# The second MoE of an attention + MoE + MoE kernel, run over its features in four parts

## The chip, the core and the metric

The kernel runs on one core of a Trainium2 chip. The metric is device time in microseconds (us). The engines are TensorE (PE, matmuls and weight loads), VectorE (DVE), ScalarE (ACT), GpSimd (POOL) and SyncE (SP, which issues most DMAs). SBUF is the on-chip memory, PSUM the accumulators of the matmuls (here 4 banks `mm` and 2 pairs of banks `s`).

## The reference, cut to what matters

Attention over 4 batches of 12 heads, 448 positions and 64 columns, then two MoE layers (1792 tokens, 768 columns, 2048 features) on its output. The weights of both MoEs come as float64, the rest as float32.

```python
q_n, k_n = rmsnorm(q, g_q), rmsnorm(k, g_k)
attn = softmax(q_n @ k_n.T / sqrt(64))         # per batch and head
x  = (attn @ v).transpose(0, 2, 1, 3).reshape(1792, 768)
h  = x @ w_in1;   x2 = (h * sigmoid(1.702 * h)) @ w_out1
h2 = x2 @ w_in2;  out = (h2 * clip(h2 + 3, 0, 6) / 6) @ w_out2
```

## The kernel before, in words

All large products run in float16 with each operand split into a high and a low half (`split`, lines 427 to 441: a high half by `scaled`, line 404, and a subtraction for the low one, line 425). A product then is three matmuls: high by high, low by high, high by low (`PROD`).

**Order.** Every step is an `op` of a planner (`Plan`): a set of engines on which it may run with a cost in ns, the steps that it depends on, and leases of buffers from rings. `order()` simulates the engines, picks by rank, and writes one fixed order for each engine; `off`, `pw` and the other constants in `CFG` shift the ranks. At run time each engine goes through its list in order. The matmuls of the MoEs follow one another in program order by a chain of dependencies (`last[0]`). Where the planner foresees a longer gap on PE it puts matmuls of no use into it (line 1488).

**Stages.** For batch 0 the attention runs first, with the weights of the first MoE loaded and decoded beside it. Then for each batch b: its inward product (`add_in1`, line 1218: 16 feature blocks of 128, 448 columns each, 18 matmuls a block), the attention of batch b+1 beside it (`add_norm`, `add_units`; scores in lines 1011 and 1014, products with V in line 972), and its outward product (`add_out1`, line 1271), whose result x2 goes to DRAM (`x2d`). The norm of batch b+1 uses the same SBUF (`arena`) as the turned exponentials of batch b, so it starts after the products with V of batch b. In the trace the inward products run at full pace from about 161, 355, 529 and 695 us, and the second MoE from 808 us.

**Decoding a float64 weight** (`decoded`, lines 496 to 557): one piece of 768 or 1024 values per partition is loaded raw (`wr`, ring of 2), POOL takes the sign (line 525), DVE puts in the low mantissa bits (532), POOL or ACT rebias the high word (516, 521), DVE puts it in (539), giving float32 in `wc` (ring of 2). ACT squares it for its size, DVE makes a scale of it, and `split` writes the halves.

**The second MoE's weights** (`Parked`, lines 605 to 681) are decoded like that while batches 1 to 3 are worked on, 12 pieces of 1024 for w_in2 and 16 of 768 for w_out2, by rows of 128 inputs (one scale per input row and partition). The halves are stored to DRAM (`park`), and loaded back whole into `wa` and `wb`, the homes of the first MoE's weights, once the last batch's products have read those (`add_back`).

**The second MoE** takes 5 chunks of 384, 384, 384, 384 and 256 tokens. Per chunk: x2 is loaded from DRAM and split (`add_x2`, line 1354), 16 feature blocks go inward (line 1218), ACT computes the gate (1364), DVE multiplies (1367) and splits g into `gt` (high half in 410, low in 425). Then for each 128 tokens all 16 features go outward into a pair of PSUM banks (line 1385: 96 matmuls of 384 columns), and ACT or DVE copy both halves out (1404), which are stored.

Of the kernel before, what the change touches and what calls it, by code (L numbers as in the profile page):

```python
# [34 lines left out]
    pw=[1850, 3255, 5600, 4119],  # L35
    pn=[2931, 3150, 2550, 4100],
    ps=[2514, 2461, 2150, 4173],
# [5 lines left out]
    off=[2000, 6000, 10500, -18500, -50000, 30000, -10000, -3000, -3000, 21500, -4500, -12000, -7500, -10000, -43000, -7500, -2000, -2000, -20000, 0],  # L43
    abias=1400,
    cuts=[],
    bias0=[0, 200, 500, 300, 0],
    bias1=[0, 600, 900, 0, 0],
    dlook=1000,
    warm=9,
    late=800,  # L50
    idle=1000,
)
# [52 lines left out]
class Ring:  # L105


    def __init__(self, n, ordered=True):
        self.held, self.ordered, self.made, self.given = [None] * n, ordered, 0, 0

# [3 lines left out]
    def when(self, lease):  # L114

        if self.ordered and lease.turn != self.given:
            return None
        free = [(0.0 if l is None else l.free, i) for i, l in enumerate(self.held) if l is None or not l.todo]
        return min(free) if free else None


class Lease:
    def __init__(self, ring, readers=1):
        self.ring, self.left, self.turn = ring, readers, ring.made
        ring.made += 1


class Op:
# [3 lines left out]
    def __init__(self, ways, deps, takes, gives, dma):  # L132
        self.ways, self.takes, self.gives, self.dma = ways, takes, gives, dma
        self.deps = [d for d in deps if d is not None]
        self.also, self.soft, self.off, self.slack = [], None, 0.0, 0.0
        self.succ, self.rank = [], 0.0


class Plan:
# [48 lines left out]
    def order(self):  # L188
# [5 lines left out]
        for o in self.ops:  # L194
            o.missing, o.ready = len(o.deps), [0.0] * 5
            for l in o.also + [x for x in (o.takes, o.gives) if x is not None]:
                l.todo, l.free, l.slot = l.left, 0.0, None
                l.ring.reset()
# [3 lines left out]
        for _ in self.ops:  # L202
            best = None
            for e in range(5):
                can = []
                for o in wait[e]:
                    r = o.ready[e]
                    if o.takes is not None:
                        free_at = o.takes.ring.when(o.takes)
                        if free_at is None:  # L210
                            continue
                        if free_at[0] + CFG['late'] * (e == PE) > r:
                            r = free_at[0] + CFG['late'] * (e == PE)
# [19 lines left out]
            if o.takes is not None:  # L233
                ring = o.takes.ring
                o.takes.slot = ring.when(o.takes)[1]
                ring.held[o.takes.slot] = o.takes
                ring.given += 1
# [30 lines left out]
    def keep_busy(self, t0, t1):  # L268
# [4 lines left out]
        held = self.spare.held  # L273
# [15 lines left out]
def attention_moe_moe_kernel(ctx, tc, q, k, v, g_q, g_k, w_in1, w_out1, w_in2, w_out2, out):  # L289
    nc = tc.nc  # L290
    B, NH, S, D = q.shape
    NT, DM = out.shape
    DF = w_in2.shape[1]
# [7 lines left out]
    CHUNKS = (384, 384, 384, 384, 256)  # L301
# [10 lines left out]
    def tiles(name, n, shape, dt):  # L312
        return [sb.tile(shape, dt, name=f"{name}{i}") for i in range(n)], Ring(n)

    wa = sb.tile([128, 2, KD, DF], F16, name="wa")
    wb = sb.tile([128, 2, KF, DM], F16, name="wb")
    gt = sb.tile([128, 2 * KF * S], F16, name="gt")
    xt = sb.tile([128, 2, KD, S], F16, name="xt")
    arena = sb.tile([128, 12 * TB * 128], F16, name="arena")
    pt = arena.rearrange("p (s t c) -> p s t c", s=12, t=TB)  # L320
    wr_t, wr_ring = tiles("wr", 2, [128, 1024], I64)
    wc_t, wc_ring = tiles("wc", 2, [128, 1024], I32)
    wbf = wb.rearrange("p e k c -> p (e k c)")

    w1_t, w1_ring = [wbf[:, 10752 + 1536 * i:12288 + 1536 * i].bitcast(I32) for i in range(8)], Ring(8)
    st_t, st_ring = tiles("st", NST, [128, S], F32)
    st_ring.ordered = False
    vr = sb.tile([128, 2, TB, D], F32, name="vr")
    vr_t, vr_ring, pair_ring = [vr[:, i] for i in range(2)], Ring(2), Ring(1)
    qkt_t, qkt_ring = tiles("qkt", 4, [128, 21, 64], F16)  # L330

    vhl, vhl_ring = sb.tile([128, TB, 4, D], F16, name="vhl"), Ring(1)
    bot_t, bot_ring = tiles("bot", 1, [128, S], F16)
    ident16 = sb.tile([128, 128], BF16, name="ident16")
    p_t, p_ring = tiles("p", 8 - NST, [128, S], F32)
    phl, phl_ring = tiles("phl", 2, [128, 2, TB, 128], F16)
    p_ring.ordered = phl_ring.ordered = False
    mm_t, mm_ring = [ps.tile([128, 512], F32, name=f"mm{i}") for i in range(NMM)], Ring(NMM, False)
    s_t, s_ring = [ps.tile([128, 2, 512], F32, name=f"s{i}") for i in range(4 - NMM // 2)], Ring(4 - NMM // 2)
    xd = [dram.tile([KD, 128, 2 * S], F16, name=f"xd{i}") for i in range(2)]  # L340
# [3 lines left out]
    smalls = sb.tile([128, 716], F32, name="smalls")  # L344
# [99 lines left out]
    three = small()  # L444
# [10 lines left out]
    def gains():  # L455
        nc.sync.dma_start(out=gq_t, in_=g_q.unsqueeze(0).to_broadcast([128, D]))
        nc.sync.dma_start(out=gp, in_=g_k.unsqueeze(0).to_broadcast([128, D]))
        nc.gpsimd.memset(three, 3.0)
# [14 lines left out]
    class Weight:  # L473
# [22 lines left out]
        def decoded(self, src, raw, cl, release):  # L496
# [5 lines left out]
            stage = lambda: wr_t[raw.slot].bitcast(F16)[:, :2 * n].rearrange("p (e n) -> p e n", e=2)  # L502
# [44 lines left out]
            done = dict(gives=raw) if release else {}  # L547
# [9 lines left out]
            return c, stage, o  # L557

        def add(self, i, m, after):
# [3 lines left out]
            for j in range(i, i + m):  # L563
                raw, cl = Lease(wr_ring), Lease(self.c_ring)
                flat, _, o = self.decoded(self.src[j], raw, cl, True)
# [39 lines left out]
    class Parked(Weight):  # L605

        def __init__(self, src, inward):
            self.src, self.inward = src, inward  # L610
            self.wide = src.dtype == I64
            self.rows = KD if inward else KF
            self.parts = 2 if inward else 1
            self.n = src.shape[1] // self.parts
            self.sq, self.s = small(self.rows * self.parts), small(self.rows)
            self.e, self.fac, self.emax, self.big_e = small(self.rows), small(self.rows), small(), small()
            self.park = dram.tile([128, 2, self.rows, src.shape[1]], F16, name="park_in" if inward else "park_out")
            self.loads, self.stores, self.scaled = [], [], []
            self.c_t = wc_t

        def add(self, i):
            n, s, e = self.n, self.s[:, i:i + 1], self.e[:, i:i + 1]
            squares, pieces = [], []
            for j in range(self.parts):
                raw, cl = Lease(wr_ring), Lease(wc_ring)
                c, stage, o = self.decoded(self.src[128 * i:128 * i + 128, j * n:j * n + n], raw, cl, False)
                sq = self.sq[:, i * self.parts + j:i * self.parts + j + 1]

                def square(c=c, stage=stage, sq=sq):
                    nc.scalar.activation(out=stage()[:, 0], in_=c(), func=AF.Square, accum_out=sq)  # L630

                squares.append(op((ACT, t_act(n, 1) + 45, square), [o]))
                pieces.append((c, stage, raw, cl))
            m = self.sq[:, i * self.parts:i * self.parts + 1]

            def scale():
                if self.parts == 2:
                    nc.vector.tensor_tensor(out=m, in0=m, in1=self.sq[:, 2 * i + 1:2 * i + 2], op=ALU.add)
                root_exponent(e, m)
                inverse(s, e, 13)  # L640

            o = op((DVE, 480 if self.parts == 1 else 630, scale), squares)
            self.scaled.append(o)
# [778 lines left out]
    for j, n in enumerate(CHUNKS):  # L1422
        chunks.append(Chunk(j, c0, n))
        c0 += n
# [104 lines left out]
```

## Time and profile before

| | before |
|---|---|
| median of 3 runs | 1239.22 us (1237.36 to 1239.52) |
| span of the profiled execution | 1245.9 us |
| PE busy | 1145.1 us (92%) |
| DVE busy | 757.2 us (61%) |
| ACT busy | 705.1 us (57%) |
| POOL busy | 393.6 us (32%) |
| mean granted TensorE clock | 0.977 |

The profiled execution has no time of its own beside its span; the span is 6.7 us over the median of the timed runs. Busy time of PE contains matmuls that wait inside the pipeline, so it is compared with counts of matmuls below. In the rows "in_moe_w_in_dram" and "in_moe_w_out_dram" stand for the weights of both MoEs; 1024-value pieces of w_in and 768-value pieces of w_out belong to the second.

### The profile page before, as it was taken

Reading aid. Unit: us, or ns where it says so; the run is one execution under the profiler, and the core shown is the slowest. Engines: PE = TensorE matmul, PEld = TensorE weight load, DVE = VectorE, ACT = ScalarE, POOL = GpSimd, SP = SyncE. Lnnn points to the kernel's source line nnn. Section 1 sums busy time; section 2 is a strip of 40 time slices with the busy share of each in tenths; the row PEclk is TensorE's granted clock in tenths of the full one; section 3 lists DMA queues with packets and bytes.
Section 4 is the critical chain, followed back from the end, with each engine's and each line's share of the span. In section 5 each row is a group of like instructions: output and inputs, shape, how many; then the busy total and the mean of one; then the engine's idle time right before and its main releaser. Section 6 shows DMA issues by size and latency. Waiting matters only on the chain.

```text
span 1245.9 us, 19206 instructions
## 1 busy us (share of the span) xinstructions
PE 1145.1 (92%) x7151; PEld 654.0 (52%) x7151; DVE 757.2 (61%) x1326; ACT 705.1 (57%) x1512; POOL 393.6 (32%) x340
## 2 busy tenths in 40 slices
PE   2888898889797999989998899999999999999998
PEld 0555544444353455435454455566666666666684
DVE  7998799989889977699768775451041041041040
ACT  3888767888857787557778665541141141141140
POOL 6656667674747323456311221200000000000000
PEclk9999799999999999989999999999999999999999
DMA  6775567799986799866799876470100100100101
GB/s 177 209 192 175 175 193 205 170 193 221 224 261 185 186 193 229 262 188 191 155 193 247 240 252 225 137 215 14 47 18 13 46 19 14 40 12 13 26 1 26
DMA packets 253182, 180.05 MB, mean 145 GB/s; under 512 B 195488, under 2 KB 240544, under 8 KB 250016
## 3 DMA queue, kind: packets, MB, share of 16 engines
q1 hardware_dynamic: 251904, 177.66, 54.7%
q10 hardware_dynamic: 1184, 1.16, 0.4%
q8 instruction: 56, 0.92, 0.3%
q14 instruction: 38, 0.31, 0.1%
HBM read 96.01 MB, written 37.36 MB: 107 GB/s over the span
## 4 chain that ended last, share of the span: by engine, by line
PE 56%; DVE 8%; DMA 4%; issue 3%; ACT 2%; POOL 2%; SPq 1%; ACTq 0%; DVEq 0%; POOLq 0%
PE mm L1218 23%; PE s L1385 18%; PE mm L1271 10%; DMA arena<-phl 2%; PE mm L972 2%; DVE phl L425 1%; PE s L1011 1%; PE s L1014 1%; DVE smalls L782 1%; DMA arena<-in_q_dram 1%; POOL phl L440 1%; DVE arena L836 1%; DVE gt L425 1%; DVE st L1252 1%; ACT p L1024 1%
## 5 line engine op out<-in xcount | busy, mean ns | idle before, releaser
L1218 PEld LDWEIGHTS <-wa 128*128 128x128 f16 x2592 | 255.4, 99 | 193.4 <-issue 15.7
L1271 PE MATMUL mm<-gt,wb 128*128 128x448 f16 x1152 | 231.8, 356 | 10.1 <-POOL wb L440 4.0
L1218 PE MATMUL mm<-xt,wa 128*128 128x448 f16 x1152 | 231.0, 359 | 8.3 <-DVE st L1252 5.4
L1218 PE MATMUL mm<-arena,wa 128*128 128x384 f16 (+1 forms) x1440 | 219.6, 315 | 0.0
L1385 PE MATMUL s<-wb,gt 128*128 128x384 f16 x1344 | 219.2, 326 | 0.0
L1367 DVE SCALAR_TENSOR_TENSOR st<-st,mm 128x384 f32<-128x384 f32 (+1 forms) x80 | 42.1, 527 | 250.3 <-ACT st L1364 250.3
L1385 PEld LDWEIGHTS <-gt 128*128 128x128 f16 x1344 | 131.5, 98 | 86.8
L1271 PEld LDWEIGHTS <-wb 128*128 128x128 f16 x1152 | 112.6, 99 | 119.2 <-issue 6.1
L425 DVE SCALAR_TENSOR_TENSOR gt<-st,smalls,gt 128x448 f16<-128x448 f32 (+2 forms) x144 | 102.5, 717 | 51.7 <-ACT gt L410 50.5
L1024 ACT ACTIVATE p<-s,smalls 128x448 f32<-128x448 f32 x168 | 120.9, 721 | 17.6 <-DVE phl L425 6.6
L1404 ACT ACTIVATE p<-s,smalls 128x384 f32<-128x384 f32 x28 | 14.7, 577 | 199.6 <-PE s L1385 126.8
L410 ACT ACTIVATE gt<-st,smalls 128x384 f16<-128x384 f32 (+2 forms) x132 | 81.5, 621 | 78.3 <-DVE st L1367 46.0
L1019 DVE TENSOR_REDUCE smalls<-s 128x2 f32<-128x896 f32 (+1 forms) x96 | 92.0, 964 | 20.2 <-PE s L1014 19.7
L416 POOL TENSOR_SCALAR arena<-p,smalls 128x384 f16<-128x384 f32 (+1 forms) x13 | 9.9, 761 | 280.5 <-DMA p<-x2d 192.1
L1011 PE MATMUL s<-qkt 128*128 128x448 f16 (+1 forms) x192 | 62.9, 371 | 34.5 <-ACT p L1024 27.5
L1364 ACT ACTIVATE st<-mm,smalls 128x384 f32<-128x384 f32 (+1 forms) x80 | 51.7, 648 | 65.8 <-PE mm L1218 62.9
L425 DVE SCALAR_TENSOR_TENSOR phl<-p,smalls,phl 128x448 f16<-128x448 f32 x90 | 76.4, 875 | 9.6 <-ACT phl L410 5.7
L525 POOL TENSOR_SCALAR wc<-wr 128x1024 f32<-128x1024 f32 (+1 forms) x40 | 45.1, 1128 | 103.2 <-DMA wr<-in_moe_w_out_dram 75.2
L532 DVE SCALAR_TENSOR_TENSOR wc<-wr,wc 128x1024 uint32<-128x1024 uint32 (+1 forms) x40 | 46.9, 1171 | 31.7 <-POOL wc L525 31.7
L1014 PE MATMUL s<-qkt 128*128 128x448 f16 (+1 forms) x192 | 62.4, 366 | 0.0
L440 POOL TENSOR_TENSOR phl<-p,phl 128x448 f16<-128x448 f32 x31 | 43.4, 1409 | 49.4 <-ACT phl L410 43.4
L1073 PE MATMUL mm<-vhl,p 128*128 128x128 f32 x336 | 48.2, 299 | 9.5 <-ACT arena L1083 4.0
(165 smaller groups left out, 1566.1 us busy)
## 6 DMA issues: line engine op xcount, KB each, us to landing
wr<-in_moe_w_in_dram SPq DMA_DIRECT2D x16, 768.0 KB, 4.9
wr<-in_moe_w_out_dram SPq DMA_DIRECT2D x12, 1024.0 KB, 6.2
wr<-in_moe_w_in_dram SPq DMA_DIRECT2D x12, 1024.0 KB, 6.7
wr<-in_moe_w_out_dram SPq DMA_DIRECT2D x16, 768.0 KB, 4.7
qkd<-arena SPq DMA_DIRECT2D x18, 672.0 KB, 3.9
park_in<-wr SPq DMA_DIRECT2D x12, 512.0 KB, 4.4
park_out<-wr SPq DMA_DIRECT2D x16, 384.0 KB, 3.3
wa<-park_in SPq DMA_DIRECT2D x4, 1536.0 KB, 8.9
```

The costliest lines, as they stand in the source:

```text
L410: nc.scalar.activation(out=dst(), in_=src(), func=AF.Copy, scale=s)
L425: nc.vector.scalar_tensor_tensor(out=dst(), in0=src(), scalar=s, in1=high(), op0=ALU.mult, op1=ALU.subtract)
L440: (POOL, t_pool2(n), lambda: nc.gpsimd.tensor_tensor(out=lo(), in0=src(), in1=hi(), op=ALU.subtract)),
L1011: nc.tensor.matmul(o, lhsT=x[:, 64 * t:64 * t + m], rhs=x[:, 448:896], start=True, stop=False)
L1014: nc.tensor.matmul(o, lhsT=x[:, 64 * t:64 * t + m], rhs=x[:, 896:1344], start=False, stop=True)
L1019: nc.vector.tensor_reduce(out=nb, in_=s_t[sl.slot][:, :m, :S], axis=AX.X, op=ALU.max)
L1024: nc.scalar.activation(out=p(i), in_=s_t[sl.slot][:, i, :S], func=AF.Exp, bias=nb[:, i:i + 1], scale=alpha, accum_out=z[:, i:i + 1],)
L1073: nc.tensor.matmul(mm_t[tl.slot][:, 128 * j:128 * j + 128], lhsT=p(i)[:, c:c + 128], rhs=diag(), start=True, stop=True,)
L1218: nc.tensor.matmul(mm_t[ml.slot][:, :n], lhsT=w.inw(we, kc, f), rhs=x[:, xe, kc, :n], start=(kc == 0 and i == 0), stop=(kc == KD - 1 and i ...
L1271: nc.tensor.matmul(mm_t[ml.slot][:, :S], lhsT=W2.outw(we, fc, d * 128, 128), rhs=gv[:, ge_, fc, :], start=(fc == g.part.start and i == 0), ...
L1364: nc.scalar.activation(out=t, in_=m, func=AF.Relu, scale=ch.c3, bias=three)
L1385: nc.tensor.matmul(s_t[sl.slot][:, h, :half], lhsT=g[:, ge_, fc, tb * 128:tb * 128 + 128], rhs=W4.outw(we, fc, h * half, half), start=(fc ...
```

## The change

The second MoE runs over its 2048 features in four parts of 512 (`PARTS` of `PART` = 4 blocks). For each part all 1792 tokens are visited in chunks of 512, 512, 512 and 256. x2 is split once and stays in SBUF for all parts (`x_all`, in the place of `wa`). The outward product of a part is a partial sum: ACT copies it into `acc` (in the place of `wb`) for part 0, DVE adds to `acc` for parts 1 to 3, and the output is stored in part 3.

The weights are no longer parked in DRAM. `Streamed` decodes one part (4 pieces of 768 of w_in2 and 4 of w_out2) into one of two targets, during the part before; part 0 is decoded before the second MoE starts. Its w_in2 pieces may be loaded and brought to 32 bits (ring `uc` of 4) once w_out1 is decoded; its targets lie where the attention worked and are free after the last batch's products with V (`last_users`). w_in2 now is cut by feature blocks (reordered on the host by a reshape), so a scale belongs to a feature; one matmul per part spreads the joint scales of its 8 pieces (`join_scales`).

On PE the outward product of a visit follows the inward product of the next one. Tiles were laid out anew so that these buffers share places, and the planner's constants differ.

```diff
-    CHUNKS = (384, 384, 384, 384, 256)
+    CHUNKS = (512, 512, 512, 256)
...
-    class Parked(Weight):
...
-            return sp(128 * 4 * self.rows * n, load, self.stores + after)
+    PART, PARTS = 4, KF // 4
+    ur_t, ur_ring = row(wr_m, 0, 2, [128, LINE], I64)
+    uc_t, uc_ring = row(wr_m, 12288, 4, [128, LINE], I32)
+    w3_t = [cut(xt_m, 10752, [128, PART, 2, KD, 128], F16), cut(gt_m, 16384, [128, PART, 2, KD, 128], F16)]
+    w4_t = [cut(p_m, 0, [128, PART, 2, DM], F16), cut(gt_m, 28672, [128, PART, 2, DM], F16)]
+    class Streamed:
+        def add(self, part, after, free):
...
+                o = sp(128 * n * (8 if self.wide else 4), load, after, takes=raw)
+                if self.wide:
+                    x = op((POOL, 1.33 * n, sign), [o], takes=cl)
+                    x = op((DVE, t_dve_bits(n), decode_a), [x])
+                    o = op([(POOL, 1.6 * n, rebias_pool), (ACT, t_act(n), rebias_act)], [x])
+                    o = op((DVE, t_dve_bits(n), decode_b), [o])
+                squares.append(op((ACT, t_act(n, 1) + 45, square), [o], gives=raw))
...
+                _, self.done[i] = split(
+                    lambda e, i=i: self.dst(i, e), lambda c32=c32: c32().bitcast(F32), self.s[:, i:i + 1], n,
+                    [o] + free, gives=cl, pool=spread(i, KF, CFG['rw'][2 if self.left else 3]),
+                )
...
+    x_all = cut(wa_m, 0, [128, 2, KD, NT], F16)
+    acc = cut(wb_m, 0, [128, NT // 128, DM], F32)
...
+        def leave(self, wdone, acc_free):
...
+                    if part == 0:
+                        o = op((ACT, t_act(half, 1), first), [last[0], self.sized] + acc_free, gives=sl)
+                    else:
+                        o = op((DVE, t_dve(half) + 85, add), [last[0], added[at, h]], gives=sl)
...
-        if b == 0:
-            for i in range(W3.rows):
-                W3.add(i)
-            W3.add_scales(1.0)
...
+    W3.add(0, sum([w.done for w in (W2,)], []), last_users)
+    W4.add(0, [], last_users)
+    for part in range(PARTS):
+        for j, ch in enumerate(chunks):
+            here = Visit(ch, part, len(visits), joined)
+            here.enter(visits[-2].left_ if len(visits) > 1 else acc_free)
+            visits.append(here)
+            if len(visits) > 1:
+                u = visits[-2]
+                u.leave(None, acc_free)
...
+            if j == 0 and part + 1 < PARTS:
+                W3.add(part + 1, [], [before.entered] if part else acc_free)
+                W4.add(part + 1, [], [before.left] if part else acc_free)
+                following = join_scales(part + 1)
```

## Rows read from the trace of the kernel before

**Rows 1.** The page: its head.

```profile
span 1245.9 us, 19206 instructions
```

**Rows 2.** Windows by stage: length, busy of each engine (instructions), granted clock, DMA.

```profile
355.00:529.00 174.00, 161.99 (x1032) 83.94 (x1031) 145.02 (x239) 126.78 (x290) 77.90 (x64) 0.97 0.88 221
529.00:695.00 166.00, 150.76 (x975) 78.75 (x974) 134.57 (x245) 119.69 (x273) 59.74 (x55) 0.97 0.84 197
695.00:808.00 113.00, 112.50 (x602) 58.87 (x602) 68.02 (x137) 67.02 (x111) 25.28 (x23) 1.00 0.64 215
808.00:1246.00 438.00, 432.23 (x2753) 269.18 (x2751) 102.13 (x195) 118.32 (x198) 7.07 (x9) 1.00 0.13 36
```

**Rows 3.** Windows, two undisturbed stretches of PE.

```profile
748.00:779.00 31.00, 31.00 (x166) 16.05 (x164) 15.50 (x28) 16.32 (x28) 5.83 (x6) 1.00 0.68 226
841.00:872.00 31.00, 31.00 (x193) 18.66 (x191) 4.69 (x8) 6.19 (x10) 0.00 (x0) 1.00 0.06 14
```

**Rows 4.** Timeline of PE: start, length, line, [idle before].

```profile
524.70 4.69 PE L1488 MATMUL mm<-ident 128*128 128x512 bf16 x21
...
801.21 6.01 PE L1218 MATMUL mm<-arena,wa 128*128 128x384 f16 x36
```

**Rows 5.** Windows of line 972, the products with V, by stage.

```profile
529.00:695.00 166.00, 17.34 (x286) 13.21 (x286) 0.97 0.84 197
```

**Rows 6.** Waits of PE from 355 to 695 us: total, times, longest.

```profile
PE s L1011 <- DMA qkt<-qkd: 5.5, 1, 5.5
PE mm L1218 <- DVE st L1252: 4.4, 1, 4.4
```

**Rows 7.** Windows by stage of tile wr, raw weights: DVE, ACT, POOL.

```profile
355.00:529.00 174.00, 29.28 (x22) 11.03 (x16) 22.07 (x15) 0.97 0.88 221
529.00:695.00 166.00, 22.72 (x20) 18.59 (x26) 12.00 (x9) 0.97 0.84 197
695.00:808.00 113.00, 32.98 (x33) 34.08 (x50) 20.22 (x17) 1.00 0.64 215
```

**Rows 8.** Chain of waits in order of time: start, length, what.

```profile
368.35 1.55 DVE wc L532
489.29 7.69 DMA arena<-phl
693.78 0.96 DVE wc L532
```

**Rows 9.** Groups by form: decoding, 355 to 695, then 748 to 800 us.

```profile
L425 DVE SCALAR_TENSOR_TENSOR wr<-wc,smalls,wr 128x1024 f16<-128x1024 f32 x7 | 10.4, 1493 | 0.5 <-POOL wr L416 0.5
...
L539 DVE SCALAR_TENSOR_TENSOR wc<-wr,wc 128x768 int32<-128x768 int32 x7 | 7.3, 1040 | 1.3 <-ACT wr L521 0.8
L425 DVE SCALAR_TENSOR_TENSOR wr<-wc,smalls,wr 128x768 f16<-128x768 f32 x5 | 5.6, 1127 | 4.7 <-ACT wr L410 4.7
L390 DVE TENSOR_SCALAR smalls<-smalls 128x1 int32<-128x1 int32 x7 | 1.1, 153 | 7.0 <-ACT wr L630 7.0
L410 ACT ACTIVATE wr<-wc,smalls 128x768 f16<-128x768 f32 x5 | 4.7, 935 | 2.7 <-DVE smalls L399 2.6
```

**Rows 10.** Groups by form: 529 to 600 us, 748 to 800 us, the page.

```profile
L425 DVE SCALAR_TENSOR_TENSOR gt<-st,smalls,gt 128x448 f16<-128x448 f32 x16 | 13.1, 828 | 1.1 <-POOL gt L416 1.1
...
L425 DVE SCALAR_TENSOR_TENSOR gt<-st,smalls,gt 128x448 f16<-128x448 f32 x2 | 1.4, 677 | 0.0
L532 DVE SCALAR_TENSOR_TENSOR wc<-wr,wc 128x768 uint32<-128x768 uint32 x7 | 6.7, 956 | 16.8 <-POOL wc L525 16.8
...
L425 DVE SCALAR_TENSOR_TENSOR phl<-p,smalls,phl 128x448 f16<-128x448 f32 x90 | 76.4, 875 | 9.6 <-ACT phl L410 5.7
```

**Rows 11.** Waits of SP's queue from 355 to 695 us.

```profile
SPq L509 <- DMA park_in<-wr: 7.2, 5, 2.5
```

**Rows 12.** Groups by form from 808 to 1246 us.

```profile
L1367 DVE SCALAR_TENSOR_TENSOR st<-st,mm 128x384 f32<-128x384 f32 x64 | 35.3, 554 | 196.2 <-ACT st L1364 196.2
```

**Rows 13.** Waits over the span.

```profile
DVE wc L532 <- POOL wc L525: 31.7, 18, 5.9
```

More of the change, by code (lines that the diff above doesn't have):

```diff
@@ L195, in order @@
             o.missing, o.ready = len(o.deps), [0.0] * 5
-            for l in o.also + [x for x in (o.takes, o.gives) if x is not None]:
+            for l in o.also + o.takes + ([] if o.gives is None else [o.gives]):
                 l.todo, l.free, l.slot = l.left, 0.0, None
@@ L232, in order @@
                 wait[w[0]].remove(o)
[L233 to L237, printed above, removed]
+            for l in o.takes:
+                l.slot = l.ring.when(l)[1]
+                l.ring.held[l.slot] = l
+                l.ring.given += 1
             o.way = way
@@ L309, in attention_moe_moe_kernel @@
     queue = lambda: nc.scalar if plan.queue else nc.sync
[L312 to L319, printed above, removed]
+    wa_m = sb.tile([128, 2 * KD * DF], F16, name="wa")
@@ L603, in outw @@
             return wb[:, e, fc, d0:d0 + n]
-    class Parked(Weight):
[L609 to L643, printed above, removed]
-            for j, (c, stage, raw, cl) in enumerate(pieces):
-                _, l = split(lambda k, stage=stage: stage()[:, k], c, s, n, [o], gives=cl, pool=spread(
-                    i * self.parts + j, self.rows * self.parts, CFG['rw'][self.number]))
-                def store(j=j, stage=stage):
-                    queue().dma_start(out=self.park[:, :, i, j * n:j * n + n], in_=stage())
-                self.stores.append(sp(128 * n * 4, store, [l], gives=raw))
-        def add_scales(self, f):
-            lease = Lease(mm_ring)
-            e16 = self.emax.bitcast(BF16)[:, :1]
-            row = lambda: mm_t[lease.slot][:, :128]
-            def largest():
-                nc.vector.tensor_reduce(out=e16, in_=self.e, axis=AX.X, op=ALU.max)
-            def spread_out():
-                nc.tensor.matmul(row(), lhsT=e16.to_broadcast([128, 128]), rhs=ident16, start=True, stop=True)
-            def scales():
-                nc.vector.tensor_reduce(out=self.big_e, in_=row(), axis=AX.X, op=ALU.max)
-                inverse(self.emax, self.big_e, 0)
-                times(self.fac, self.e, self.emax, f)
-            o = op((DVE, 200, largest), self.scaled)
-            o = op((PE, 300, spread_out), [o], takes=lease)
-            self.big = op((DVE, 700, scales), [o], gives=lease)
-        def add_back(self, j, k, after):
-            n = self.src.shape[1] // k
-            here = (wa if self.inward else wb)[:, :, :, j * n:j * n + n]
-            def load():
-                queue().dma_start(out=here, in_=self.park[:, :, :, j * n:j * n + n])
-            return sp(128 * 4 * self.rows * n, load, self.stores + after)
@@ L1362, in add_in2 @@
[L1362 to L1384 removed]
+            self.bs = [batches[b] for b in range(c0 // S, (c0 + n - 1) // S + 1)]
@@ new lines, in gate, with product @@
+                def gate(t=t, m=m, c=c, k3=k3):
+                    nc.scalar.activation(out=t(), in_=m(), func=AF.Relu, scale=c, bias=k3)
+                def product(t=t, m=m, k6=k6):
+                    nc.vector.scalar_tensor_tensor(out=t(), in0=t(), scalar=k6, in1=m(), op0=ALU.min, op1=ALU.mult)
+                o = op((ACT, t_act(n, 2) - 50, gate), [last[0], self.sized], takes=tl)
+                o = op((DVE, t_dve(n), product), [o], gives=ml)
+                o = op(scaled(hi, t, 1.0, n), [o] + g_after)
```

414 lines of the change are left out of this document (283 added, 131 removed).

## The prediction, made before the change was run

> **What bounds the kernel now.** I read the head of the page first [rows 1]: the profiled span is 1245.9 us, 6.7 us over the median of the timed runs, 1239.2, so sums are made against the span and 6.7 us come off at the end. In the windows by stage [rows 2] PE looks like the bound everywhere, but the ends of its matmuls are modelled, so I compared what a stage takes with what its matmuls need at full rate. Full rate is read where nothing disturbs it [rows 3]: 166 matmuls of 448 columns in 31.0 us are 186.7 ns each, 193 of 384 columns 160.6 ns, both 0.417 to 0.418 ns a column.
>
> The second MoE runs at that rate: 1152 + 1344 + 288 matmuls of 384 and 256 columns are 2 x 516,096 columns, 431.7 us, and PE is busy 432.2 in the last stage of 438. The last batch's first MoE does too: 576 x 186.7 = 107.5 us in a stage of 113 that also holds 36 matmuls of the next one (6.0 us) [rows 4]. The two stages from 355 to 695 us don't. Each holds one batch's first MoE (107.5), the next batch's scores (96 matmuls, 17.9) and its products with V (17.3 in the dearer stage [rows 5]): 142.7 us of PE in 174 and 166. That is 54.6 us too much. PE there waits for q/k transposes and DVE's gate product [rows 6], or runs filler matmuls ahead of an inward block [rows 4].
>
> DVE is the reason that I can show: busy 145.0 of 174 and 134.6 of 166 [rows 2]. 52.0 us of that (29.3 + 22.7) are instructions on the raw tile of the second MoE's weights [rows 7], and the chain of waits goes through them by name: between 355 and 695 it has 21 pieces of that decoding, 25.4 us, of which the first and the last stand in [rows 8]; three small scale instructions on DVE beside them add about 3.
>
> **The change, part by part.** *Decoding leaves the attention stages.* DVE loses there the 52.0 us and the small ones, three of 0.153 us for each of 13 pieces [rows 9], 6.0: 58. What comes back is part 0 of w_in2, which has to wait for its target until the last batch's products with V and can only be decoded to 32 bits: four pieces with two passes of 0.96 [rows 10] and 1.04 us [rows 9] and 0.46 of scales, 8.5 us. So DVE needs 279.6 - 58 + 8.5 = 230 us in two stages where PE needs 285.4. The 60.4 us in which DVE now stands idle there are waits for other engines and DMAs. If all of them stay, the stages take 230 + 60.4 = 290.5. If the chain alone shortens, they take 340 - 25.4 - 3 + 8.5 = 320. If all comes off, PE's 285.4 remain. I take 295, near the DVE sum and above it, since two engines would now be near their limit at once: 45 us won, bounds 20 and 55. ACT (126.8 + 119.7, of which 29.6 go) and POOL (77.9 + 59.7, of which 34 go) lose work too and stay under DVE.
>
> A side of this is weighed with the Trainium skill. The row: the same low-half subtraction of 128x448 takes 828 ns from 529 to 600 us, with POOL busy, and 677 from 748 to 800 us [rows 10]. The Trainium skill, "SBUF — State Buffer", section "Who interferes with whom", says that a DVE instruction with two SBUF inputs and a GpSimd instruction that reads SBUF exclude each other for the whole instruction. By that rule the attention's own subtractions would become shorter when POOL loses a quarter of its work there: 32 gate instructions with 0.15 and two thirds of the 90 split ones with 0.20 us too much are 17 us, a quarter of which is an estimated 4 us, and the sum would be 1189. The rows alone show the difference, not its cause, so my sum goes without it.
>
> *The queue.* SP is in order. From 355 to 695 it stood 7.2 us at weight loads whose buffer a parked store still held, with DMA transposes behind them [rows 11]. 28 stores and 6 loads back go. This runs beside the DVE term and is not added to it.
>
> *The stage from 161 to 355* decodes w_out1, and that stays. Two pieces of w_in2 fall into it, each with three passes on DVE, the longest of them 1.49 us, and 0.46 of scales [rows 9]: at most 10 us. Bounds 0 and 10, and I take 5. The new constants of the planner shift the order of all loads; no row prices that, and I put it at 0 with 10 to either side.
>
> *695 to 808.* Here PE has no gap to win. DVE is busy 68.0 of 113, 33.0 of it on the decoding of w_out2 [rows 2, 7]. Afterwards it has four pieces of w_out2 (4 x 3.5 = 14), four subtractions for w_in2 (4.4) and those for x2 (some 17) instead: no more than now. x2's first chunk needs batches 0 and 1 only, and the third chunk, which needs the last batch, is entered three blocks of 15.4 us later. 0.
>
> *The second MoE.* The columns stay 2 x 516,096, so PE's need stays 430.2 to 431.7. DVE gets 84 additions for parts 1 to 3, beside the 28 evacuations that ACT keeps for part 0. An addition reads PSUM and SBUF as the gate product does, 0.55 us [rows 12]: 47 us. Gate products and subtractions keep their columns and stay inside the 102 of now. 24 pieces with 0.96 + 1.04 + 1.13 + 0.46 [rows 9, 10]: 86. 16 visits with three to four scale instructions, some 1 us: 16. Together 251 of 432 us. ACT goes from 118 to some 190: 24 pieces with three passes of 0.94 [rows 9] are 68. All of this lies beside matmuls. What could let it through is the PSUM ring: a feature block of 512 columns takes PE 3.85 us, and with four banks the next three blocks are 11.5 us, against some 1.5 us for gate and product (0.74 for the product in proportion [rows 12], as much for the gate). 24 loads of 768 KB in 330 us are 57 GB/s on DMA engines that are 13% busy there [rows 2]. The matmuls that spread scales stand in PE's queue and wait for eight pieces; I put one wait of about 1 us at each of four parts, well under the single waits in [rows 6], 4 us. At the end two additions (1.1 us) and a store follow the last matmul, where two copies and stores half as large follow now: at most 1 us, inside the 4.
>
> Sum: 1245.9 - 45 - 5 + 4 = 1199.9 of span; less 6.7 is **1193 us**.
>
> **Rivals.** *Only the chain's own pieces go* (17 in 100). The attention stages are a sequence of scores, maximum, exponential, split, transpose, and the last one ends behind DMA transposes of up to 7.7 us [rows 8]; for it speaks that PE's idle and filler time gathers at the ends of batches. Then 20 us are won there and none in the first stage: 1239.2 - 20 + 4 = 1223. Against it: DVE is over 80% busy and runs in order, so every piece taken out moves what is behind it.
>
> *All of it goes, and more* (19). The stages reach PE's need (55 us), and the first stage, 194 us for the same 142.7, gives 20 because w_out1 gets the raw tiles to itself and SP and POOL are freer: 1239.2 - 55 - 20 + 2 = 1166. Against it: w_out1's decoding isn't touched.
>
> *DVE's order lets the streaming through to PE* (10), the case on the other side. DVE executes in order. A first decoding pass that waits for its load and for POOL holds up the gate product behind it, and with it a PSUM bank. Such waits exist: from 748 to 800 us DVE stood 16.8 us before 7 of these passes, 2.4 each [rows 10], and the longest such wait in the run is 5.9 [rows 13]. In a chunk of 256 columns three blocks cover only 5.8 us less some 1 of gate and product. If every one of 24 pieces cost PE its 2.4 us, that is 58: 1193 - 4 + 58 = 1247. It decides from 1.9 us a piece (46 over 24). Against it: the same pieces run today from 695 to 808 beside matmuls, and those lost nothing.
>
> *The decoding still comes early* (2): the planner could load and decode parts 1 to 3 before the attention ends. Four buffers for 32-bit pieces hold part 0 until the last products with V, so it can't go further; no change then, 1239.
>
> My forecast has 52.
>
> **How the numbers follow.** The forecast's own range is 1176 (55 and 10 won, 2 lost) to 1214 (30 won, 5 lost). The range reaches to most of the case of all gains and past that of the chain: 1150 to 1228. Outside are the streaming rival (10), part of the case of all gains (5) and the fourth with some remainder (5). A difference of 0.2%, about 2.5 us, is what runs of this kernel can tell. Slower: 9 of the streaming rival's 10. No change: the early decoding 2, and 2 from the border of the others. Faster: 87.
>
> **What would show it.** Right: stages of about 147 us between inward blocks where 174 and 166 stand; DVE some 25 us less busy in each; no decoding in the chain before the last batch; PE busy in the whole second MoE with waits of at most a few us, DVE at about half. Wrong: PE waits on the gate product or on weights in the second MoE, gaps at the part changes, a lower granted clock there than the 1.00 of now [rows 2], or attention stages as long as before with DVE less busy, which would make them a chain of latencies.

## The result, and the profile after

The changed kernel takes 1193.1 us in the median (1190.0 to 1195.4), the kernel before on the same chip 1239.4 (1237.4 to 1242.9): a ratio of 0.961, 95% interval 0.957 to 0.965. The forecast was 1193 us.

The head of the page, against [rows 1]; the span is 55.2 us shorter:

```profile
span 1190.7 us, 18317 instructions
```

The windows by stage, against [rows 2], with the first stage ahead: length, busy of PE, PEld, DVE, ACT, POOL (instructions), granted clock, share of the DMA engines, GB/s. The edges from 342 us on are the ends of the four batches' outward products.

```profile
161.00:342.00 181.00, 155.87 (x980) 80.35 (x978) 160.69 (x264) 135.94 (x307) 124.67 (x96) 0.93 0.80 199
342.00:491.00 149.00, 144.75 (x965) 76.14 (x964) 109.85 (x196) 114.03 (x269) 45.76 (x49) 0.99 0.82 186
491.00:634.00 143.00, 140.29 (x903) 73.00 (x902) 109.09 (x203) 103.41 (x247) 46.36 (x47) 0.99 0.78 176
634.00:748.00 114.00, 113.76 (x644) 60.13 (x643) 62.87 (x125) 54.15 (x93) 17.89 (x18) 1.00 0.29 97
748.00:1191.00 443.00, 437.22 (x2507) 244.92 (x2505) 222.76 (x395) 145.25 (x237) 56.18 (x44) 1.00 0.16 51
```

These edges are not those of [rows 2], which lie where an inward product came to full pace. By such instants (342.2, 490.6 and 642.4 us) the two attention stages take 148 and 152 us where 174 and 166 stood. Between the ends of outward products, the measure of the table below, they take 148.5 and 143.6 where 151.6 and 163.9 stood, and the last batch 113.9 where 131.9 stood, because the attention of before ran on into the next batch. PE now is busy in nearly all of both stages. The second MoE keeps its length although DVE works 222.8 us in it instead of 102.1.

PE's timeline where batches meet (start, length, line, with [idle before] where there is any) shows it. In both kernels an inward product starts as the outward one ends. In the kernel before it then broke off for filler [rows 4] and for the late products with V of its own batch (line 972), 11 us after it had started in batch 2 and 20 in batch 3:

```profile
505.45 3.00 PE L1218 MATMUL mm<-xt,wa 128*128 128x448 f16 x15
...
516.50 3.12 PE L972 MATMUL mm<-arena,vhl 128*64 128x128 f16 x55
...
689.27 3.19 PE L972 MATMUL mm<-arena,vhl 128*64 128x128 f16 x55 [1.62 <-DMA arena<-phl]
```

In the changed kernel these products (line 1062) end ahead of batch 2's inward product and 6 us behind the start of batch 3's, no filler is left behind 342 us, and the second MoE starts as the last outward product ends:

```profile
486.31 3.21 PE L1062 MATMUL mm<-xt,gt 128*64 128x128 f16 x55 [0.25 <-DMA xt<-p]
489.45 1.31 PE L1361 MATMUL mm<-gt,wb 128*128 128x448 f16 x6
490.60 2.43 PE L1308 MATMUL mm<-xt,wa 128*128 128x448 f16 x12
...
631.73 2.62 PE L1361 MATMUL mm<-gt,wb 128*128 128x448 f16 x13
634.19 3.00 PE L1308 MATMUL mm<-xt,wa 128*128 128x448 f16 x15
637.12 3.12 PE L1062 MATMUL mm<-xt,gt 128*64 128x128 f16 x55
...
642.36 7.92 PE L1308 MATMUL mm<-xt,wa 128*128 128x448 f16 x41 [0.21 <-DVE smalls L423]
...
743.76 4.51 PE L1361 MATMUL mm<-gt,wb 128*128 128x448 f16 x23
748.11 4.26 PE L1479 MATMUL mm<-wa,xt 128*128 128x512 f16 x19
```

PE's waits from 340 to 1190 us (total, times, longest), against [rows 6], are these three; the 5.5 us for the transposes and the 4.4 us for the gate product are gone, and none lies in the second MoE. Over batches 1 to 3 PE's waits were 27.2 us in the profile shown (24.8 in the second profile of the kernel before) and are 7.1; filler matmuls took 17.4 us there (17.3) and now take none.

```profile
PE s L1101 <- ACT p L1114: 6.7, 2, 4.0
PE mm L1062 <- DMA xt<-p: 0.2, 1, 0.2
PE mm L1308 <- DVE smalls L423: 0.2, 1, 0.2
```

The raw tile's instructions by the same windows (length, DVE, ACT, POOL, clock, DMA), against [rows 7]: 6 us of DVE are left in the two attention stages where 52 were (45 between the ends of outward products), and 67.3 have moved into the second MoE.

```profile
342.00:491.00 149.00, 5.96 (x5) 4.59 (x8) 3.19 (x3) 0.99 0.82 186
491.00:634.00 143.00, 0.00 (x0) 0.00 (x0) 0.00 (x0) 0.99 0.78 176
634.00:748.00 114.00, 28.10 (x27) 20.48 (x31) 15.96 (x15) 1.00 0.29 97
748.00:1191.00 443.00, 67.31 (x60) 47.89 (x74) 50.83 (x36) 1.00 0.16 51
```

The page's groups that answer to [rows 12] and [rows 10]: the additions to `acc`, the gate product, and the low-half subtraction of the turned exponentials (mean ns after the busy time).

```profile
L1529 DVE SCALAR_TENSOR_TENSOR wb<-s,smalls,wb 128x384 f32<-128x384 f32 x84 | 48.1, 613 | 88.2 <-PE s L1513 88.1
L1494 DVE SCALAR_TENSOR_TENSOR wa<-wa,smalls,mm 128x512 f32<-128x512 f32 (+1 forms) x64 | 43.4, 678 | 77.6 <-ACT wa L1491 77.3
L458 DVE SCALAR_TENSOR_TENSOR p<-p,smalls 128x448 f16<-128x448 f32 x90 | 71.0, 821 | 17.4 <-ACT p L443 15.6
```

### The profile page after: what moved, and what is told of

It is laid out like the page before. It is cut to its first block, busy times and chain, and to the rows that moved or that the text cites. A ratio compares the mean times of both kernels' runs of the same rounds, so it can differ in the third digit from the quotient of the medians.

```text
span 1190.7 us, 18317 instructions
## 1 busy us (share of the span) xinstructions
PE 1108.2 (93%) x6748; PEld 610.0 (51%) x6748; DVE 804.2 (68%) x1426; ACT 678.6 (57%) x1469; POOL 408.4 (34%) x362
## 4 chain that ended last, share of the span: by engine, by line
PE 67%; DVE 15%; DMA 5%; ACT 5%; POOL 4%; issue 4%; SPq 0%; DVEq 0%; POOLq 0%; ACTq 0%
PE s L1513 18%; PE mm L1479 18%; PE mm L1361 15%; PE mm L1308 7%; PE mm L1062 3%; PE s L1101 2%; PE s L1104 2%; DMA xt<-in_q_dram 2%; DVE gt L458 1%; DVE smalls L1109 1%; DVE smalls L872 1%; DMA xt<-p 1%; ACT p L1114 1%; PE mm L1029 1%; PE mm L1163 1%
## 5 line engine op out<-in xcount | busy, mean ns | idle before, releaser
L1513 PEld LDWEIGHTS <-gt 128*128 128x128 f16 x1344 | 131.6, 98 | 87.3
L1308 PEld LDWEIGHTS <-wa 128*128 128x128 f16 x1152 | 114.0, 99 | 118.3 <-issue 18.1
L1513 PE MATMUL s<-p,gt 128*128 128x384 f16 x672 | 110.8, 326 | 0.0
L1513 PE MATMUL s<-gt 128*128 128x384 f16 x672 | 110.5, 326 | 0.0
L1479 PE MATMUL mm<-wa,gt 128*128 128x512 f16 (+1 forms) x576 | 110.3, 352 | 0.0
L1479 PE MATMUL mm<-wa,xt 128*128 128x512 f16 (+1 forms) x576 | 110.2, 352 | 0.0
L1101 PE MATMUL s<-gt 128*128 128x448 f16 (+1 forms) x192 | 64.4, 382 | 23.5 <-ACT p L1114 20.7
L1479 PEld LDWEIGHTS <-gt 128*128 128x128 f16 x576 | 56.3, 98 | 52.1
L1479 PEld LDWEIGHTS <-xt 128*128 128x128 f16 x576 | 56.2, 98 | 52.1
L458 DVE SCALAR_TENSOR_TENSOR p<-p,smalls 128x448 f16<-128x448 f32 x90 | 71.0, 821 | 17.4 <-ACT p L443 15.6
L443 ACT ACTIVATE p<-p,smalls 128x448 f16<-128x448 f32 (+1 forms) x96 | 60.2, 659 | 9.6 <-DMA xt<-p 6.4
L1104 PE MATMUL s<-gt 128*128 128x448 f16 (+1 forms) x192 | 64.3, 378 | 0.0
L458 DVE SCALAR_TENSOR_TENSOR gt<-wa,gt 128x512 f16<-128x512 f32 (+1 forms) x64 | 42.0, 658 | 25.5 <-ACT gt L443 25.4
```

Of the source, the lines that this page charges most:

```text
L443: nc.scalar.activation(out=dst(), in_=src(), func=AF.Copy, scale=s)
L458: nc.vector.scalar_tensor_tensor(out=dst(), in0=src(), scalar=s, in1=high(), op0=ALU.mult, op1=ALU.subtract)
L1101: nc.tensor.matmul(o, lhsT=x[:, 64 * t:64 * t + m], rhs=x[:, 448:896], start=True, stop=False)
L1104: nc.tensor.matmul(o, lhsT=x[:, 64 * t:64 * t + m], rhs=x[:, 896:1344], start=False, stop=True)
L1308: nc.tensor.matmul(mm_t[ml.slot][:, :n], lhsT=w.inw(we, kc, f), rhs=x[:, xe, kc, :n], start=(kc == 0 and i == 0), stop=(kc == KD - 1 and i ...
L1479: nc.tensor.matmul(mm_t[ml.slot][:, :n], lhsT=W3.inw(we, kc, f), rhs=x_all[:, xe, kc, ch.c0:ch.c0 + n], start=(kc == 0 and j == 0), stop=( ...
```

## The experiments

All runs are compared by the instants at which the outward products of the four batches and the last matmul end. The lengths between them are in us and come from one profiled execution of each kernel; the first column is an instant, and ratios are to the kernel before on the same chip:

| run | batch 0 ends | batch 1 | batch 2 | batch 3 | second MoE | median, ratio (95%) |
|---|---|---|---|---|---|---|
| before, profile shown | 354.0 | 151.6 | 163.9 | 131.9 | 438.8 | 1239.4 |
| before, once more | 345.6 | 152.2 | 162.5 | 129.7 | 438.9 | 1236.4, one run |
| after | 342.3 | 148.5 | 143.6 | 113.9 | 436.9 | 1193.1, 0.961 (0.957 to 0.965) |
| e1 old structure, new constants | 348.5 | 144.6 | 165.0 | 127.0 | 467.2 | 1259.5, 1.014 (1.009 to 1.019) |
| e2 new structure, old constants | 355.8 | 147.2 | 143.2 | 113.6 | 436.9 | 1204.5, 0.970 (0.967 to 0.974) |
| e3 decoding again | 341.7 | 143.0 | 160.1 | 131.6 | 436.9 | 1225.0, 0.986 (0.982 to 0.990) |
| e4 loads again | 342.2 | 143.8 | 164.2 | 113.7 | 436.8 | 1208.2, 0.973 (0.969 to 0.977) |
| e5 DVE passes again | 339.0 | 147.8 | 148.2 | 143.8 | 436.9 | 1223.4, 0.985 (0.981 to 0.988) |
| e6 two banks | 341.3 | 150.6 | 144.5 | 113.9 | 442.5 | 1198.5, 0.963 (0.960 to 0.966) |
| e7 w_out1 without DVE passes | 323.2 | 158.7 | 148.9 | 113.7 | 436.9 | 1190.2, 0.956 (0.953 to 0.959) |
| e9 48 reductions, same order | 342.0 | 159.2 | 148.7 | 113.9 | 436.9 | 1208.8, 0.974 (0.971 to 0.978) |
| e11 24 reductions | 345.1 | 153.6 | 144.5 | 113.9 | 437.0 | 1198.3, 0.966 (0.964 to 0.969) |
| e10 48 in the second MoE | 342.1 | 149.3 | 145.2 | 113.9 | 447.3 | 1204.1, 0.971 (0.969 to 0.973) |
| e12 three engines, same order | 344.9 | 160.3 | 155.0 | 113.9 | 436.9 | 1216.3, 0.980 (0.977 to 0.984) |

**The kernel before, once more.** No edit.

> The kernel before, profiled a second time: its first profile had a span 6.7 us over the median of its runs. If that profile is typical in its stages, batches end again near 354, 506, 670 and 801 us; if the surplus lies in one place, it is gone there and the span is near 1238.

Its profiled span is 1234.6 us, 11.3 less than that of the profile shown, and 8.4 of these lie ahead of the end of batch 0. So these two executions of one kernel differ most in the first stage, and its length alone proves little below some 10 us. Behind it executions agree better: e10 leaves batches 1 to 3 of the changed kernel as they are, and they take 408.4 us where 406.0 stand for the changed kernel. Against the second execution of before the change won 3.3 us in the first stage, 3.7, 18.9 and 15.8 in batches 1 to 3, 2.0 in the second MoE and 0.2 behind it: 43.9. Batches 1 to 3 together went from 444.4 to 406.0, by 38.4 (by 41.4 against the profile shown).

**Structure and constants apart.** e1 is the kernel before with the new planner constants, e2 the changed one with the old:

```diff
-    pw=[1850, 3255, 5600, 4119],
-    pn=[2931, 3150, 2550, 4100],
+    pw=[226, 922, 5600, 4119],
+    pn=[5844, 7048, 2259, 9380],
...
```

> The kernel before with the changed kernel's planner constants (those of the parked weights kept). Theory: the gain of 46 us comes from taking the second MoE's decoding off DVE in the attention stages, so constants alone leave the time near 1239, 1227 to 1250. Rival: the new constants order the attention better and make most of the gain; then it is 1215 or less.

> The changed kernel with the old planner constants for the stages up to the last batch: paces, biases, and the offsets of the values, the norms, the units and the inward products (those of the first batch's norm and units, of the first MoE's weights and of the outward product have to stay new, since no order exists otherwise). Theory: the move itself carries the gain, 1193 to 1212. Rival (constants): 1222 or more.

e2 came as the theory had it: with the old constants batches 1 to 3 take 404.0 us, no more than with the new ones, so what was won there is the structure's. The first stage is 13.5 us longer with them, near to the whole difference of 11. e1 missed both expectations. The new constants shorten batches 1 to 3 of the old structure by 7.8 us and put a hole of 30 us into the start of its second MoE. PE's timeline of e1 there (first two lines) shows it full of filler matmuls, and the chain of waits (last line) goes through them alone:

```profile
784.94 6.01 PE L1218 MATMUL mm<-arena,wa 128*128 128x384 f16 x36
...
790.93 29.51 PE L1488 MATMUL mm<-ident 128*128 128x512 bf16 x136
```

```profile
791.07 29.38 PE mm L1488 x136
```

So the profile shows nothing that PE waited for there; the planner had foreseen a gap and filled it, and the 136 useless matmuls are the loss. Without the 28.3 us by which its second MoE is longer e1 would be at an estimated 1231, inside the theory's range. Constants fitted to one structure are no neutral part of a comparison.

**Decoding, loads and DVE passes put back, with the planner's order made anew.** Each kernel is the changed one with 16 pieces of unused work between w_out1's decoding and part 0: e3 decodes them in full, e4 only loads them, e5 only runs three DVE passes of 768 values and the small scale instructions for each, spread over batches 1 and 2.

```diff
-    W3.add(0, sum([w.done for w in (W2,)], []), last_users)
+    again = [extra(i) for i in range(KF)]
+    W3.add(0, sum([w.done for w in (W2,)], []) + again, last_users)
```

> The changed kernel, with the 16 pieces of w_in2 loaded, decoded and split once more between the end of w_out1's decoding and the last attention, and thrown away: some 56 us of DVE, 25 to 45 of ACT and POOL, 12.6 MB of loads, no parking stores. Theory (DVE's decoding work is what the attention stages lose): most of the 40 us that the two attention stages gained are lost again, 1213 to 1238. Rival (the stages are a chain of latencies, or the gain is that of the parked stores and the loads back): 1203 or less.

> The changed kernel with only the 16 loads of the run before put into the same stages, 12.6 MB into the raw buffers, nothing computed from them. Theory (DVE): nothing to see, 1190 to 1200. Rival (traffic of the DMA queue, whose transposes the attention waits for): 1208 or more.

> The changed kernel with the DVE share of the decoding alone put back into the stages of batches 1 and 2: 16 times three passes over 768 values and the two scale instructions, some 53 us of DVE, on a 32-bit buffer, no loads, nothing on POOL or ACT, each group released by a matmul of the stage (its values are used by nobody). The run with all of the decoding put back lost 30 us, the one with the loads alone 14, of which 13.2 are one wait behind a late store. Theory (DVE): 1210 to 1235, spread over the stages. Rival (the order of SP's queue and the transfers make the loss, DVE's work little): 1203 or less.

e3 gives back 28.7 us of the 38.4 in batches 1 to 3, with the profile of before: batch 1 cheap, 2 and 3 dear. e4 went against the theory by its number, but not by the transposes that the rival had named: 13.2 of its 15.7 us are one wait of PE (first line), and the chain of waits that leads to it (start, length, what) goes through the store of x2. That store stood in SP's queue behind transposes (line 1175) and weight loads (line 664), and ACT needed its buffer `st`.

```profile
PE mm L1112 <- ACT mm L1446: 13.2, 1, 13.2
```

```profile
493.48 0.51 SPq L1175
...
494.79 0.59 SPq L664
...
495.43 5.21 DMA x2d<-st
...
500.66 0.65 ACT st L1427
...
501.81 0.20 ACT mm L1446
...
502.05 4.00 PE mm L1112 x20
```

e5 met its number, but between the ends of outward products batches 1 and 2, where the passes are, lose 3.9 us together and batch 3 loses 29.9. That is an attention that ended late: from the last product with V of batch 1 to that of batch 3 pass 341.8 us in e5, 340.6 in the kernel before, once more, and 307.6 in the changed one. Whether DVE's passes did that isn't isolated: they took turns in the ring of part 0's buffers, so that its real decoding starts at 634.8 us (336.5 in the changed kernel), and the planner made another order. Such runs change order and queues along with the load, so they can't say what DVE's time alone is worth.

**Engine time put back, with no order changed.** In e9, e11, e10 and e12 every engine keeps the changed kernel's order. Only reductions of 128x8x128 values into a private buffer come between DVE's instructions (e12: and small products on POOL and squares on ACT between theirs), from batch 1's first inward block to the last products with V; in e10 from the second visit of the second MoE to its last.

```diff
-        for o in self.done:
...
+        for i, o in enumerate(self.done):
             o.way[2]()
+            if i0 <= i < i1 and o.way[0] == DVE:
+                k += 1
+                if k % 7 == 0 and n < 48:
+                    n += 1
+                    self.more()
```

> The changed kernel with every engine's order as it stands, and 48 reductions of no use on DVE (128x8x128 bf16, an estimated 1.1 us each, some 50 us in all), one after every 7th DVE instruction from batch 1's first inward block to the last batch's products with V. They share no buffer with anything and no other engine gets an instruction. Theory (DVE's time is what the attention stages gained): 24 us more DVE work per stage brings back 15 to 35 us, all of it before the second MoE, so 1208 to 1228 us. Rival (what the runs with added decoding lost came from the planner's other order, from buffers and from SP's queue): at most 1201 us.

> The same with 24 reductions, one after every 14th DVE instruction (some 26 us). Theory: about half of the loss of the run with 48, or somewhat less since PE's and DVE's needs then are closer: 1200 to 1212 us. Rival: at most 1197 us.

> The changed kernel with its order, and on three engines as much time of no use as the change took from them between batch 1's first inward block and the last batch's products with V: the 48 DVE reductions of before (58 us, 1208.8 us by themselves), 88 POOL products of 64 columns (an estimated 50 us) and 114 ACT squares of 64 columns (an estimated 30 us). No transfer, no buffer shared, no other order. If the engines' time is what the stages gained, the kernel comes back to 1220 to 1240 us. Rival (a good part of the gain is in the transfers and in what the decoding's instructions wait for, not in the engines' time): at most 1215 us.

Group of the reductions and windows of batches 1 to 3 in e9; then the same windows in the kernel before, once more:

```profile
L1645 DVE TENSOR_REDUCE smalls<-ident 128x8 f32<-128x1024 bf16 x48 | 58.0, 1208 | 0.0
...
342.00:501.00 159.00, 147.41 (x960) 77.07 (x959) 134.46 (x218) 113.12 (x267) 46.85 (x49) 0.97 0.76 174
501.00:650.00 149.00, 141.51 (x909) 73.53 (x907) 132.23 (x229) 103.85 (x250) 43.10 (x47) 0.98 0.74 169
650.00:764.00 114.00, 113.76 (x644) 60.09 (x643) 62.82 (x125) 54.70 (x93) 18.36 (x18) 1.00 0.30 98
```

```profile
346.00:498.00 152.00, 142.62 (x904) 73.47 (x902) 132.10 (x219) 116.89 (x271) 70.23 (x57) 0.98 0.90 213
498.00:660.00 162.00, 152.45 (x957) 78.79 (x956) 129.75 (x224) 112.93 (x256) 64.73 (x58) 0.97 0.82 203
660.00:790.00 130.00, 123.90 (x714) 65.53 (x713) 83.48 (x167) 79.50 (x141) 28.07 (x27) 0.99 0.72 228
```

e9's DVE is as busy in batches 1 and 2 as that of the kernel before (134.5 and 132.2 against 132.1 and 129.8), but they cost 15.8 us, not 38.4, and batch 3 stays at PE's need. Half of the reductions (e11) cost 6.0 in batches 1 to 3, over twice the 2.4 between two executions; the median of 1198.3 falls between the two ranges. So DVE's time is a cause, at 0.2 to 0.3 us per us, and e9 met the theory's range at its low end. e12 adds 36.2 us on POOL and 28.7 on ACT. In batches 1 and 2 DVE, ACT and POOL then are busy 265, 241 and 123 us where they were 262, 230 and 135 in the kernel before, once more. The cost rises to 23.2 us, and the median, 1216.3, falls between the rival's 1215 and the theory's 1220. Its groups:

```profile
L1654 POOL TENSOR_TENSOR smalls<-gp 128x64 f16<-128x64 f32 x88 | 36.2, 411 | 3.5
L1657 ACT ACTIVATE smalls<-gp 128x64 f16<-128x64 f32 x114 | 28.7, 251 | 2.4
```

So some 60% of what was won in batches 1 to 3 (23.2 of 38.4) comes back with engine time. The other 15.2 us do not, and no run here isolates them. Two things that e12 lacks can be read in the chain of the kernel before, once more, where batches 2 and 3 start:

```profile
503.68 4.43 PE mm L1488 x14
...
676.01 5.38 DMA wr<-in_moe_w_out_dram
681.54 0.90 POOL wc L525
682.46 0.96 DVE wc L532
683.42 0.55 DVE xt L1110
684.00 0.35 PE mm L1218
```

The first is the planner's filler. PE's waits in batches 1 to 3 are 26.0 us in e12 and 24.8 in the kernel before, once more; what e12 lacks are the 69 filler matmuls, 17.3 us. 14 of them stand in the chain themselves: as far as the profile shows nothing else held PE in these 4.4 us. The others fill time in which something else was late.

The second is what a pass waits for. PE waited for `xt`, the attention's result. DVE had that subtraction of 0.55 us in its order behind a decoding pass, and the pass waited for a weight of 5.4 us and for POOL's sign. DVE stood idle for 1.1 us before the pass, which no busy time shows. How much of the 15.2 us each of the two is wasn't isolated, since transfers and the planner's order changed with them.

**The second MoE's cover.** e6 lets its inward product use two of the four `mm` banks; e10 puts e9's 48 reductions there.

```diff
-                ml, tl = Lease(mm_ring), Lease(t_ring)
+                ml, tl = Lease(mm_ring, most=2), Lease(t_ring)
```

> The changed kernel with two PSUM banks in place of four for the inward products of the second MoE, so that one block (3.85 us) covers gate, product and whatever DVE does before them, not three. Theory: the streaming fits between the gate products with much to spare, under 6 us more, 1192 to 1200. Rival (DVE's order lets the decoding through to PE, and four banks just cover it): 1215 or more.

> The same 48 reductions, but put in the second MoE, one after every 5th DVE instruction from its second visit to its last. Theory: DVE is busy half of that stage and four PSUM banks cover a delay of 1.1 us, so at most 4 us are lost: 1192 to 1198 us. Rival (DVE's in-order queue lets delays through to PE there): 1205 us or more.

e6: 5.6 us, inside the theory's range. e10 fell between the two: 10.4 us more in the second MoE, 7.4 of it two waits of PE's outward product for DVE's addition, the longer one in the timeline below. The 48 matmuls behind that wait took 10.51 us, at a granted clock of 0.75 from 905.4 to 915.9 us, where such 48 take 7.96 without a wait ahead of them, so the wait of 6.4 us cost about 9:

```profile
905.38 10.51 PE L1521 MATMUL s<-gt 128*128 128x384 f16 x48 [6.42 <-DVE wb L1537]
```

The windows say why a stage with DVE at half isn't half free. First e10 around that wait, with 6 reductions in it (7.3 us), then the same stretch in the changed kernel, where it lies 2 us earlier, and then a busier one there, 11 us before it:

```profile
875.00:907.00 32.00, 25.58 (x131) 12.74 (x130) 30.92 (x55) 16.79 (x29) 7.37 (x6) 0.95 0.31 107
```

```profile
873.00:905.00 32.00, 32.00 (x175) 16.89 (x174) 25.24 (x45) 14.28 (x24) 8.62 (x6) 1.00 0.39 124
...
862.00:894.00 32.00, 32.00 (x171) 16.50 (x169) 28.72 (x54) 20.14 (x34) 12.87 (x10) 1.00 0.41 138
```

Where a part's pieces are decoded, DVE is 90% busy for 32 us already without the reductions. The addition, last in line, holds one of only two pairs of `s` banks.

**w_out1 without DVE's two passes** (24 passes, 37.0 us of DVE, less in the first stage; neither the low nor the high word is put in, so only the signs of its weights are left).

```diff
-                x = op((DVE, t_dve_bits(n), decode_a), [x])
+                if self.inward:
+                    x = op((DVE, t_dve_bits(n), decode_a), [x])
...
-                o = op((DVE, t_dve_bits(n), decode_b), [o], **done)
...
+                if self.inward:
+                    o = op((DVE, t_dve_bits(n), decode_b), [o], **done)
```

> The changed kernel without the two DVE passes that put the mantissa of the first MoE's outward weights together (12 pieces, 24 passes of 1.2 to 1.4 us; the weights lose their low bits, the rest is unchanged). Theory: the stage before 342 us is bound by DVE as the later ones were, and gives back 15 to 30 us, 1164 to 1180. Rival (a chain of latencies there): under 8 us, 1186 or more.

By its total it fell on the rival's side, by the stage that it is about on the theory's: the first stage is 19.1 us shorter, over twice the 8.4 by which two executions of the kernel before differ there, and batches 1 and 2 are 10.2 and 5.3 longer. The planner made another order for it, so why that was given back isn't shown.

## Why the prediction was right, step by step

- *Attention stages, -45 (bounds 20 and 55), and nothing in the last batch:* -38.4 against the second execution of before, -41.4 against the profile shown. The size held, the reason in part. I took DVE's sum plus its idle time, as if the sum set the stage and the idle stayed. DVE fell from 261.9 us in batches 1 and 2 to 218.9, but e9 gives a us of DVE back at under 0.3 us. The rest is the other engines' share (7.4) and 15.2 us that came back with neither. The case of the chain's pieces, which I had only as a rival, is probably part of them; of its 25.4 us, which I read as DVE's, some 14 are passes on DVE and the others on ACT, POOL and one load. The reading that fits these runs, though none tests it alone, is a race. Where the attention of the next batch ends after the outward product, the time behind goes to waits and filler; where it ends first, PE's need of 142.7 is what is left. The last products with V ended 14 and 23 us behind the outward product in the profile shown, and now end 1 us ahead of it and 6 behind; the stages stand 5.8 and 0.9 above PE's need, the last batch 6.4 above its 107.5.
- *First stage, -5 (0 to 10):* -3.3 against one execution of before, -11.7 against the other. The reason that I gave is not borne out: e2, which moves the same two pieces out of it but has most of the old constants, ends it at 355.8, later than either execution of before.
- *Span against median, -6.7:* right as a correction: 8.4 us of that execution's surplus over the other are in its first stage.
- *Constants at 0, 10 to either side:* e2 puts them at 11 us, just outside, and nearly all in the first stage, in the new structure.
- *Second MoE, +4:* -2.0. The single waits at part changes did not come: the trace has none. DVE is at 222.8 us where I summed 251, half of the stage, as said: the additions took 613 ns, not 550, but four of the 24 pieces were decoded before the stage, and scales, products and subtractions took less. ACT is at 145.3 where I summed some 190.
- *The total.* That it came within 0.2 us is luck. Against the second execution of before 6.6 us less than forecast were won in the attention stages and 1.7 less in the first stage, and 6.0 more in the second MoE, so that the misses nearly cancel.
- *Rivals.* Streaming getting through to PE did not happen, but its place was right: e10 shows the path at `s`, where I had priced `mm` alone. All gains and more (1166) failed in the first stage. The early decoding did not come: the raw tile has no work at all from 491 to 634 us.
- *Signs.* Stage lengths (148 and 152 us between inward products), no waits in the second MoE and DVE at half came as listed. "No decoding in the chain before the last batch" did not quite: four passes of part 0 (4.1 us) stand in it from 343 to 364 us, then none.
- *The side on subtractions.* In batches 1 and 2 the gate's went from 895 ns (32 times, the kernel before, once more) to 813, and the split ones from 864 (71 times) to 724 (78 times): some 13 us, more than the estimated 4. The Trainium skill, "SBUF — State Buffer", "Who interferes with whom", says that a DVE instruction with two SBUF inputs contends with a GpSimd instruction that reads SBUF. By that rule less POOL work would be the cause. e12 doesn't bear that out: with 36.2 us of POOL put back beside e9's load, the gate's mean is 827 against 824, and that of the split ones 692 against 709. Those POOL products are short, and buffers were laid out anew too, so the cause of the shorter time stays open.

The group of the gate's subtractions in batches 1 and 2, in the changed kernel, e9 and e12:

```profile
L458 DVE SCALAR_TENSOR_TENSOR gt<-st,smalls,gt 128x448 f16<-128x448 f32 x32 | 25.5, 813 | 1.7 <-POOL gt L449 1.6
```

```profile
L466 DVE SCALAR_TENSOR_TENSOR gt<-st,smalls,gt 128x448 f16<-128x448 f32 x32 | 26.1, 824 | 1.1 <-POOL gt L457 0.8 <-ACT gt L451 0.2
```

```profile
L467 DVE SCALAR_TENSOR_TENSOR gt<-st,smalls,gt 128x448 f16<-128x448 f32 x32 | 26.1, 827 | 1.9 <-POOL gt L458 1.7 <-ACT gt L452 0.2
```

## What to carry to other kernels

Work that depends on nothing nearby belongs in the stage whose bound it doesn't touch: 67 us of decoding on DVE cost the second MoE nothing that shows, and the stages that had held 52 of them gained 38 together with the last one. An engine's busy time does not tell what such work costs: 58 us of plain DVE time cost 15.8. Put plain time back without changing the order, and the difference to the whole gain is what went with something else, here with passes that hold what stands behind them while they wait for a load, with filler matmuls, or with the order. Look whether filler stands in the chain of waits before calling a gap a wait. Judge the cover in the new place by its busiest 30 us and its scarcest buffer, not by the mean of the stage.

## What the runs showed of the hardware that was not expected

A DVE reduction of 128x8x128 bf16 values, read from one 128x128 buffer, took 1.21 us. In e12 an ACT square of 64 columns took 251 ns where one of 448 columns takes 573, and a POOL product of 64 columns 411 ns in the mean (289 to 887, half of them under 296) where one of 448 columns takes 1.1 to 1.2 us: a short instruction is dear for its columns on both. After PE had stood idle for 6.4 us in e10, the granted clock was 0.75 for the next 10.5 us. The granted clock was 0.93 in the first stage of the changed kernel (161 to 342 us), where PE was busy 155.9 of 181 us, and 0.99 to 1.00 in all later stages, where it was busy 97% or more.
